# One shared pool of accumulator banks, the two banks of a double declared independent, and a first load in thirds

## The chip, the cores and the metric

The kernel runs on one core of one Trainium2 chip. The metric is device time in microseconds (us) of one execution; a lower time is better. Engines are named as in the profile: PE is the matrix engine (PEld its weight loads), ACT the scalar engine, DVE the vector engine, POOL the general one, SP the one that issues most transfers. Times are medians of several executions; unless said otherwise all were fast. Ratios are the mean time of one kernel's fast runs over the mean of the fast runs of the kernel before in the same rounds, so they are not quite the ratio of the medians quoted.

## The reference

Block-sparse attention (4 batches, 8 heads, 768 tokens, head size 64) feeds a two-layer network with a swish: 512 to 2048 to 512 over 3072 tokens.

```python
scores = (1/sqrt(64)) * q @ k.T                 # per batch and head, 768 x 768
scores = where(mask, scores, -1e9)              # mask: window, first/last, 3 sampled blocks of 32 per row block
attn = softmax(scores);  x = attn @ v           # x: 3072 x 512 after the heads are put side by side
h = x @ w_in                                    # 3072 x 2048
out = (h * sigmoid(beta * h)) @ w_out           # 3072 x 512
```

## The kernel before

All work is cut into nodes. A planner in the kernel (`order_of`) puts them in one order with modelled durations and a weight per kind (`BIAS`); each engine then runs its nodes in that order. So PE's order is fixed when the kernel is built. A "pair" is two heads of one batch; pairs 0 to 3 are batch 0, pair 4 is the first of batch 1. A "score group" is a run of score steps with nothing else between them in PE's order. A "change of form" is a switch of PE between 128-row and 64-row matmuls; each score group costs two, one on entry and one on the way back.

```python
SLOTS = {..., "et": 15, "xst": 7, ..., "sc": 2, "mm": 4}   # 2 doubles + 4 single banks = all 8 banks
"sc": many(psum, "sc", [P, 2, 512], FP32),      # a score step: both heads, one bank each
"mm": many(psum, "mm", [P, 512], FP32),         # all other matmul results
...
def mm(sc=sc, kc0=kc0):                         # a score step: 64-row matmuls, 1024 columns in all
    for i in range(kn):
        for hh in range(2):
            nc.tensor.matmul(at(sc)[:, hh, i*n:(i+1)*n], lhsT=kX[hh*D:(hh+1)*D, ...], rhs=qX[hh*D:(hh+1)*D, ...])
def ex(eng, sc=sc, et=et):                      # one exponential over both banks, frees the double
    nc.scalar.activation(out=at(et)..., in_=at(sc)..., func=AF.Exp, scale=SCALE)
def mk(eng, ...):                               # DVE: et *= mask
...
def hp(f=f, hb=hb):                             # hidden layer: 4 matmuls of 512 columns into one bank
def th(...): tanh on ACT;  def gm(...): (tanh + 1) * h on DVE, frees the bank
def op(...):                                    # out projection: 16 matmuls into one bank, in fours
```

Attention (24 matmuls of 65 columns per bank) is normalized by DVE into `xst`, transposed, and copied to `xT_sb`, from which hidden layers read. A hidden group covers 256 or 512 tokens: 16 nodes of four matmuls. The first full one (512 tokens) needs the attention of all four pairs of batch 0.

The softmax here doesn't subtract the row's maximum and nothing guards it: scores larger than these inputs give would overflow.

## Time and profile before

The median was 280.78 us (280.04 to 281.09, 3 runs).

| | before |
|---|---|
| PE, ACT, DVE busy, share of span | 95%, 76%, 75% |
| PE waits from 63 us to its last matmul | 0.07 us of 213.5 |
| score groups in PE's order (built order) | 78: 14 of one step, 62 of two, 2 of three |
| first exponential | 8.76 us |

From the page of the kernel before: busy time, and two rows of the span in 40 slices (in tenths; PEclk is the clock granted to PE).

```profile
PE 265.3 (95%) x2455; PEld 139.5 (50%) x2455; DVE 209.5 (75%) x424; ACT 212.9 (76%) x281; POOL 28.0 (10%) x45
...
PE   4597899999999999999999999999999999999994
...
PEclk9997799999999999999999999999999999999999
```

The table of windows of the kernel before: for each stretch its length, then busy us of each engine, the clock, the transfer share and rate.

```profile
core 0: us, PE busy (x) PEld busy (x) DVE busy (x) ACT busy (x) POOL busy (x), PEclk, DMA share, GB/s
0.00:63.00 63.00, 51.88 (x573) 31.62 (x573) 52.58 (x128) 49.10 (x67) 13.94 (x29) 0.95 0.97 207
63.00:276.50 213.50, 213.43 (x1884) 107.90 (x1882) 156.91 (x297) 163.22 (x214) 14.02 (x16) 1.00 0.45 109
276.50:280.10 3.60, 0.00 (x0) 0.00 (x0) 0.00 (x0) 0.60 (x1) 0.00 (x0) 1.00 0.20 75
25.00:31.80 6.80, 6.33 (x66) 3.71 (x64) 4.73 (x11) 5.71 (x7) 0.00 (x0) 0.50 1.17 208
```

From 63 us on PE never stops; before that it does, and for 6.8 us it ran at half clock. "Busy" is not "useful", though. PE's timeline in the full stretch (start, length, what, count) shows it:

```profile
84.12 1.89 PE L591 MATMUL mm<-w_out_sb,g 128*128 128x512 f16 x8
85.94 0.60 PE L462 MATMUL sc<-qX,kX 64*128 64x512 f16 x4
86.48 1.90 PE L591 MATMUL mm<-w_out_sb,g 128*128 128x512 f16 x8
88.31 0.60 PE L462 MATMUL sc<-qX,kX 64*128 64x512 f16 x4
88.85 1.90 PE L591 MATMUL mm<-w_out_sb,g 128*128 128x512 f16 x8
```

Eight out-projection matmuls and two score steps repeat every 2.37 us. The eight take 1.727 us (8 x 0.2159, from 48 in a row), the two score steps 0.427 us (the prediction's estimate). The 0.2 us left is put down to the entry into the 64-row form and the way back.

The list of waits (who waited for whom: us in total, times, longest):

```profile
ACT et L470 <- PE sc L462: 22.0, 39, 1.3
...
PE sc L462 <- ACT et L470: 3.0, 7, 0.9
```

The start, from the timeline of all engines. POOL casts k, DVE builds the mask from the sampled indices (`sb_f`), the mask matmul stands first in PE's order, and only then the transposes of k run:

```profile
4.23 0.82 POOL L395 CAST s_k<-st_k 128x768 f16<-128x768 f32 x1 [0.84 <-DMA st_k<-in_k_dram]
4.41 0.66 DVE L287 CAST sb_f<-sb_i 24x3 f32<-24x3 int32 x1 [0.72 <-DMA sb_i<-in_sampled_blocks_dram]
6.01 0.19 PE L294 MATMUL mm<-identity,mask 24*24 24x24 f16 x1 [2.86 <-DVE mask L289]
6.99 0.80 ACT L425 COPY kX<-mm 128x768 f16<-128x768 f16 x1 [3.05 <-PE mm L420]
```

### The profile page before, as it was taken

How to read it: one execution, taken by the hardware profiler on the slowest of the kernel's cores; microseconds unless marked ns; L12 is line 12 of the kernel's file. 1: busy time of each engine (PE TensorE's matmuls, PEld its weight loads, DVE VectorE, ACT ScalarE, POOL GpSimd, SP SyncE). 2: the span in 40 equal slices, each digit the busy share in tenths (PEclk: the TensorE clock that was granted, in tenths of full speed). 3: DMA queues.
4: the chain of work that ended last, by engine and by line, in shares of the span. 5: the costliest groups of instructions: out<-in, count | busy, mean ns of one | idle time of the engine just before them, and what ended most of it. 6: DMA issues, size and time to landing. Idle time of an engine off the chain costs nothing.

```text
span 280.1 us, 6128 instructions
## 1 busy us (share of the span) xinstructions
PE 265.3 (95%) x2455; PEld 139.5 (50%) x2455; DVE 209.5 (75%) x424; ACT 212.9 (76%) x281; POOL 28.0 (10%) x45
## 2 busy tenths in 40 slices
PE   4597899999999999999999999999999999999994
PEld 1364576654363664454563354643355554556741
DVE  5697999999995788887789998877876787733500
ACT  1689898879987898997879988879966877704611
POOL 5560010010200010231001310010000000000000
PEclk9997799999999999999999999999999999999999
DMA  7999994899602194996227986860102010011112
GB/s 204 292 251 213 202 176 115 109 305 233 163 4 37 48 247 115 303 252 150 68 70 204 266 207 86 248 104 35 39 2 77 37 49 37 0 22 75 40 55 96
DMA packets 72849, 36.65 MB, mean 131 GB/s; under 512 B 29796, under 2 KB 68724, under 8 KB 72820
## 3 DMA queue, kind: packets, MB, share of 16 engines
q1 hardware_dynamic: 69568, 32.06, 47.0%
q0 software_dynamic: 3136, 4.19, 8.6%
q8 instruction: 19, 0.31, 0.5%
q14 instruction: 10, 0.08, 0.1%
q10 hardware_dynamic: 116, 0.01, 0.0%
HBM read 27.27 MB, written 6.29 MB: 120 GB/s over the span
## 4 chain that ended last, share of the span: by engine, by line
PE 83%; ACT 7%; DVE 4%; DMA 3%; issue 2%; SPq 0%; ACTq 0%; DVEq 0%
PE mm L591 29%; PE mm L567 28%; PE mm L517 12%; PE sc L462 12%; ACT et L470 5%; DMA st_k<-in_k_dram 2%; PE mm L420 1%; DMA sb_i<-in_sampled_blocks_dram 1%; DVE g L576 1%; DVE et L479 1%; ACT t_sb L572 1%; DVE s_k L395 1%; ACT qX L425 0%; DVE s_q L395 0%; ACT kX L425 0%
## 5 line engine op out<-in xcount | busy, mean ns | idle before, releaser
L470 ACT ACTIVATE et<-sc 128x1024 f16<-128x1024 f32 x144 | 142.2, 1031 | 24.7 <-PE sc L462 22.0
L479 DVE TENSOR_TENSOR et<-et,mask 128x1024 f16<-128x1024 f16 x144 | 98.6, 695 | 20.0 <-ACT et L470 19.7
L591 PE MATMUL mm<-w_out_sb,g 128*128 128x512 f16 x384 | 93.3, 380 | 0.0
L567 PE MATMUL mm<-xT_sb,w_in_sb 128*128 128x512 f16 (+1 forms) x448 | 89.9, 349 | 0.4
L576 DVE SCALAR_TENSOR_TENSOR g<-t_sb,mm 128x512 f16<-128x512 f16 (+1 forms) x112 | 66.0, 608 | 23.3 <-ACT t_sb L572 22.2
L572 ACT ACTIVATE t_sb<-mm,beta_h_sb 128x512 f16<-128x512 f32 (+1 forms) x112 | 67.8, 649 | 12.9 <-PE mm L567 12.1
L567 PEld LDWEIGHTS <-w_in_sb 128*128 128x128 f16 x448 | 42.4, 98 | 44.5 <-issue 6.8
L591 PEld LDWEIGHTS <-g 128*128 128x128 f16 x384 | 33.7, 98 | 43.6 <-issue 11.5
L462 PE MATMUL sc<-qX,kX 64*128 64x256 f16 (+1 forms) x384 | 48.4, 342 | 4.3 <-ACT et L470 3.0
L517 PEld LDWEIGHTS <-et 128*128 128x128 f16 x1152 | 42.3, 100 | 9.2 <-issue 3.1
L517 PE MATMUL mm<-va,et 128*128 128x65 f16 x1152 | 44.5, 196 | 0.0
L462 PEld LDWEIGHTS <-kX 64*128 64x128 f16 x384 | 15.5, 96 | 26.9 <-issue 21.8
L601 ACT ACTIVATE osb<-mm 128x512 f32<-128x512 f32 x16 | 9.6, 599 | 18.9 <-PE mm L591 18.7
L527 DVE TENSOR_TENSOR xst<-mm,recip 128x256 f16<-128x256 f32 x48 | 20.1, 419 | 0.4
L395 POOL CAST s_q<-st_q 128x768 f16<-128x768 f32 (+1 forms) x10 | 8.5, 847 | 92.8 <-DMA st_q<-in_q_dram 89.5
L524 DVE RECIPROCAL recip<-mm 128x4 f32<-128x4 f32 x48 | 8.5, 178 | 5.5 <-PE mm L517 4.9
L395 POOL CAST va<-st_v 128x768 f16<-128x768 f32 x7 | 6.9, 983 | 15.4 <-DMA st_v<-in_v_dram 15.4
L395 DVE CAST s_k<-st_k 128x768 f16<-128x768 f32 x12 | 7.9, 656 | 0.7 <-DMA st_k<-in_k_dram 0.7
L395 DVE CAST va<-st_v 128x768 f16<-128x768 f32 x9 | 4.9, 546 | 1.5 <-DMA st_v<-in_v_dram 1.5
L395 POOL CAST s_k<-st_k 128x768 f16<-128x768 f32 x4 | 3.5, 875 | 20.8 <-DMA st_k<-in_k_dram 20.8
L603 DVE TENSOR_SCALAR osb<-mm 128x512 f32<-128x512 f32 x8 | 5.5, 684 | 0.0
L395 DVE CAST s_q<-st_q 128x512 f16<-128x512 f32 (+2 forms) x10 | 4.5, 454 | 0.0
(53 smaller groups left out, 44.3 us busy)
## 6 DMA issues: line engine op xcount, KB each, us to landing
st_k<-in_k_dram SPq DMA_DIRECT2D x16, 384.0 KB, 4.8
st_v<-in_v_dram SPq DMA_DIRECT2D x16, 384.0 KB, 5.3
out_dram<-osb SPq DMA_DIRECT2D x24, 256.0 KB, 2.0
st_q<-in_q_dram SPq DMA_DIRECT2D x12, 384.0 KB, 4.6
w_in_sb<-in_moe_w_in_dram POOLq DMA_DIRECT2D x2, 1024.0 KB, 12.0
w_out_sb<-in_moe_w_out_dram POOLq DMA_DIRECT2D x2, 1024.0 KB, 21.2
st_q<-in_q_dram SPq DMA_DIRECT2D x12, 128.0 KB, 4.6
xT_sb<-xst SPq DMA_TRANSPOSE x22, 2.4
```

The costliest lines, as they stand in the source:

```text
L395: e(out=at(dst)[:, :, :, 0:D] if nm == "v" else by_chunk(dst, lo, hi), in_=src)
L462: nc.tensor.matmul(at(sc)[:, hh, i * n:(i + 1) * n], lhsT=kX[hh * D:(hh + 1) * D, (kc0 + i) * P:(kc0 + i + 1) * P], rhs=qX[hh * D:(hh + 1) ...
L470: nc.scalar.activation(out=at(et).rearrange("p h q -> p (h q)"), in_=at(sc).rearrange("p h q -> p (h q)"), func=AF.Exp, bias=0.0, scale=SCALE)
L479: nc.vector.tensor_tensor(out=e, in0=e, in1=m, op=ALU.mult)
L517: nc.tensor.matmul(a[:, i, hh, :], lhsT=at(ets[kc // kn])[:, hh, at0:at0 + P], rhs=at(va)[:, hh, kc, 0:D + 1], start=(kc == 0), stop=(kc = ...
L524: nc.vector.reciprocal(out=at(rb), in_=av_ap()[:, :, :, D:D + 1])
L527: nc.vector.tensor_tensor(out=at(xs)[:, half * 2:half * 2 + 2], in0=av_ap()[:, :, :, 0:D], in1=at(rb).to_broadcast([P, 2, 2, D]), op=ALU.mult)
L567: nc.tensor.matmul(at(hb)[:, 0:n], lhsT=w_in_sb[:, c, f * P:(f + 1) * P], rhs=xT_sb[:, c, t0:t0 + n], start=(c == 0), stop=(c == NPAIR - 1))
L572: nc.scalar.activation(out=at(tb)[:, 0:n], in_=at(hb)[:, 0:n], func=AF.Tanh, bias=0.0, scale=beta_h_sb[:, f:f + 1])
L576: nc.vector.scalar_tensor_tensor(out=at(gb)[:, f, 0:n], in0=at(tb)[:, 0:n], scalar=1.0, in1=at(hb)[:, 0:n], op0=ALU.add, op1=ALU.mult)
L591: nc.tensor.matmul(at(ob), lhsT=at(gb)[:, f, ts * P:(ts + 1) * P], rhs=w_out_sb[:, f, :], start=(f == 0), stop=(f == N_FFC - 1))
L601: nc.scalar.activation(out=at(sb), in_=at(ob), func=AF.Copy, bias=0.0, scale=0.5)
```

## The change

Its intent: let score steps use any free double, up to three at once, so that they come in larger groups; let other results use any single bank; and start on the first third of k. The planner gets a pool of eight banks, chooses a bank for each node, and caps what a kind may hold. The buffers' dependency tracking works on the whole double, so every pair of accesses to different banks of a double, on different engines, is declared independent. All weights and several buffer counts were tuned again. The diff, cut to its core:

```diff
-BIAS = {"av": 39, ..., "gm": -151, "hp": 34, ...}
+BIAS = {"av": -69, ..., "gm": -727, "hp": -468, ..., "two sc": -72, ...}
+IN_PARTS = (0,)
+BANKS = ("sc", "mm")
+MOST = {"av": 8, "hp": 6, "sc": 3}
...
+    bank, held = [0.0] * (2 * slots["sc"]), {}      # in order_of: when each bank is free
...
+                b.slot, b.kind = bank_for(bank, b.pool, start), n.kind
...
+class Banks:
+    def access(self, insts, eng, banks, fresh, node=None):
+        for insts2, eng2, gen, node2, own2 in self.seen[d]:
+            if node and node2 and (node2 in before or own & own2):
+                continue
+            if eng2 != eng and not set(gen) & set(banks):
+                for a in insts:
+                    for b in insts2:
+                        self.tc.declare_no_dep(a, b, reason="the other bank of the double")
...
-    SLOTS = {"st_k": 3, "st_q": 6, "st_v": 4, ..., "va": 5, "et": 15, "xst": 7, "recip": 6, "t_sb": 5, ..., "osb": 2, "sc": 2, "mm": 4}
+    SLOTS = {"st_k": 2, "st_q": 5, "st_v": 5, ..., "va": 4, "et": 13, "xst": 5, "recip": 7, "t_sb": 6, ..., "osb": 3, "sc": 4}
...
     def at(buf):
+        if buf.pool == "mm":
+            return T["sc"][buf.slot // 2][:, buf.slot % 2]
...
+        if x in IN_PARTS:                               # first pair: k0, q, k1, k2
+            work = Buf("st_k"), Buf("s16_k")
+            for g in range(NG):
+                parts.append(add_half(x, "k", kq, g * CG, g * CG + CG, ...))
```

Most instructions after it carry one line (L208), that of the helper that records them, so they are told apart by their tiles; every accumulator is now called `sc`.

More of the change, by code (lines that the diff above doesn't have):

```diff
@@ L38, in __init__ @@
         self.start = self.done = self.on = None
-BIAS = {"av": 39, "beta": 625, "cast": 183, "dma": -860, "ex": 395, "gm": -151, "hp": 34,
-        "load": 1245, "lone sc": 160, "mask": -541, "mk": 266, "next sc": -48, "norm": 134,
-        "op": 45, "op on": 85, "osb": 304, "sc": -79, "spread": 28, "th": 302, "turn": -1220,
-        "turn cp": 47, "weights": 444, "x cp": 29, "x turn": -13}
+BIAS = {"av": -69, "beta": -455, "cast": 94, "dma": -1239, "ex": 257, "gm": -727, "hp": -468,
+        "load": 1496, "lone sc": 331, "mask": -1415, "mk": 241, "next sc": 94, "norm": -152,
+        "op": -13, "op on": -70, "osb": 284, "sc": -204, "spread": -316, "th": 422,
+        "turn": -3422, "turn cp": -88, "two sc": -72, "weights": 774, "x cp": -31,
+        "x turn": -102}
 W_GATE = (3, "k")
@@ L54, with banks_of, whole, soonest @@
 SHARED = 42.0
+BANKS = ("sc", "mm")
+MOST = {"av": 8, "hp": 6, "sc": 3}
+def banks_of(b):
+    return (2 * b.slot, 2 * b.slot + 1) if b.pool == "sc" else (b.slot,)
+def whole(bank, d, t):
+    return all(x is not None and x <= t for x in bank[2 * d:2 * d + 2])
+def soonest(bank, pool):
+    if pool == "mm":
+        return min((t for t in bank if t is not None), default=None)
+    pairs = [bank[i:i + 2] for i in range(0, len(bank), 2)]
+    return min((max(p) for p in pairs if None not in p), default=None)
+def bank_for(bank, pool, t):
+    if pool == "sc":
+        ok = [d for d in range(len(bank) // 2) if whole(bank, d, t)]
+        return min(ok, key=lambda d: max(bank[2 * d:2 * d + 2]))
+    ok = [i for i in range(len(bank)) if bank[i] is not None and bank[i] <= t]
+    def other(i):
+        return float("inf") if bank[i ^ 1] is None else bank[i ^ 1]
+    return max(ok, key=lambda i: (other(i), -i))
 def order_of(nodes, free, slots):
     free = dict(free)
-    give = {p: [(0.0, s) for s in range(n)] for p, n in slots.items()}
+    give = {p: [(0.0, s) for s in range(n)] for p, n in slots.items() if p not in BANKS}
+    bank, held = [0.0] * (2 * slots["sc"]), {}
     rows = 128
@@ L81, in order_of @@
             ok = True
+            if held.get(n.kind, 0) >= MOST.get(n.kind, 99):
+                continue
             for p, c in want.items():
+                if p in BANKS:
+                    t = soonest(bank, p)
+                    if t is None:
+                        ok = False
+                        break
+                    ready = max(ready, t)
+                    continue
                 if len(give[p]) < c:
@@ L96, in order_of @@
                         bias += BIAS["next sc"]
-                    elif sum(t <= n_start for t, _ in give["sc"]) < 2:
-                        bias += BIAS["lone sc"]
+                    else:
+                        room = sum(whole(bank, d, n_start) for d in range(len(bank) // 2))
+                        bias += BIAS["lone sc"] if room < 2 else BIAS["two sc"] if room < 3 else 0
                 key = (n_start + n.dur[e] - min(n.dur.values()) + bias, n.place)
@@ L122, in order_of @@
         for b in n.take:
+            if b.pool in BANKS:
+                b.slot, b.kind = bank_for(bank, b.pool, start), n.kind
+                held[n.kind] = held.get(n.kind, 0) + 1
+                for i in banks_of(b):
+                    bank[i] = None
+                continue
             t, b.slot = min(give[b.pool])
@@ L127, in order_of @@
             b.end = max(b.end, n.done)
-            if b.users == 0:
+            if b.users == 0 and b.pool in BANKS:
+                held[b.kind] -= 1
+                for i in banks_of(b):
+                    bank[i] = b.end + HOP
+            elif b.users == 0:
                 give[b.pool].append((b.end + HOP, b.slot))
@@ L139, in order_of, with __init__, __getattr__, call @@
     return out
+class Tap:
+    def __init__(self, eng, log):
+        self.eng, self.log = eng, log
+    def __getattr__(self, name):
+        f = getattr(self.eng, name)
+        def call(*a, **kw):
+            r = f(*a, **kw)
+            self.log.append(r.ins)
+            return r
+        return call
+class Banks:
+    def __init__(self, tc, n):
+        self.tc, self.seen = tc, [[] for _ in range(n)]
+        self.age = [0] * (2 * n)
+    def access(self, insts, eng, banks, fresh, node=None):
+        d = banks[0] // 2
+        if fresh:
+            for i in banks:
+                self.age[i] += 1
+            self.seen[d] = [x for x in self.seen[d]
+                            if any(self.age[i] - g <= 2 for i, g in x[2].items())]
+        own = node and {(b.pool, b.slot) for b in node.use if b.pool not in BANKS}
+        before = node and {m for m, _ in node.deps}
+        for insts2, eng2, gen, node2, own2 in self.seen[d]:
+            if node and node2 and (node2 in before or own & own2):
+                continue
+            if eng2 != eng and not set(gen) & set(banks):
+                for a in insts:
+                    for b in insts2:
+                        self.tc.declare_no_dep(a, b, reason="the other bank of the double")
+        self.seen[d].append((insts, eng, {i: self.age[i] for i in banks}, node, own))
 @with_exitstack
@@ L171 @@
     Q1 = 256
-    SLOTS = {"st_k": 3, "st_q": 6, "st_v": 4, "s16_k": 4, "s16_q": 2, "set": 4, "va": 5,
-             "et": 15, "xst": 7, "recip": 6, "t_sb": 5, "g": 2, "osb": 2, "sc": 2, "mm": 4}
+    SLOTS = {"st_k": 2, "st_q": 5, "st_v": 5, "s16_k": 4, "s16_q": 2, "set": 4, "va": 4,
+             "et": 13, "xst": 5, "recip": 7, "t_sb": 6, "g": 2, "osb": 3, "sc": 4}
     persist = ctx.enter_context(tc.tile_pool(name="persist", bufs=1))
@@ L183 @@
         "sc": many(psum, "sc", [P, 2, 512], FP32),
-        "mm": many(psum, "mm", [P, 512], FP32),
         "et": many(persist, "et", [P, 2, 512], FP16),
@@ L223, in emit_warm @@
                              start=True, stop=True)
+    log = []
+    pe, act, dve = Tap(nc.tensor, log), Tap(nc.scalar, log), Tap(nc.vector, log)
     def copy_on(eng):
-        return nc.scalar.copy if eng == "ACT" else nc.vector.tensor_copy
+        return act.copy if eng == "ACT" else dve.tensor_copy
     sb_i32 = persist.tile([NB, 3], mybir.dt.int32, name="sb_i32")
@@ L286, in mb @@
         def mb(eng):
-            nc.vector.tensor_copy(out=sb_f32, in_=sb_i32)
+            dve.tensor_copy(out=sb_f32, in_=sb_i32)
             for r in range(3):
-                nc.vector.scalar_tensor_tensor(out=mask_blk if r < 2 else mask16, in0=iota_j,
+                dve.scalar_tensor_tensor(out=mask_blk if r < 2 else mask16, in0=iota_j,
                                                scalar=sb_f32[:, r:r + 1], in1=mask_blk,
@@ L293, in mt @@
         def mt():
-            nc.tensor.matmul(at(tb)[0:NB, 0:NB], lhsT=mask16, rhs=identity[0:NB, 0:NB],
+            pe.matmul(at(tb)[0:NB, 0:NB], lhsT=mask16, rhs=identity[0:NB, 0:NB],
                              start=True, stop=True)
@@ L301, in km @@
             for g in range(NG):
-                nc.tensor.matmul(at(kb)[:, g * NB:(g + 1) * NB], lhsT=onehot[:, g], rhs=mask_t,
+                pe.matmul(at(kb)[:, g * NB:(g + 1) * NB], lhsT=onehot[:, g], rhs=mask_t,
                                  start=True, stop=True)
@@ L308, in bt @@
         def bt():
-            nc.tensor.transpose(out=at(bb)[:, 0:N_FFC], in_=beta_sb, identity=ident32)
+            pe.transpose(out=at(bb)[:, 0:N_FFC], in_=beta_sb, identity=ident32)
         def bh(eng):
-            nc.vector.tensor_scalar(out=beta_h_sb, in0=at(bb)[:, 0:N_FFC], scalar1=0.5,
+            dve.tensor_scalar(out=beta_h_sb, in0=at(bb)[:, 0:N_FFC], scalar1=0.5,
                                     scalar2=None, op0=ALU.mult)
         def spread(eng, g):
-            e = nc.vector if eng == "DVE" else nc.gpsimd
+            e = dve if eng == "DVE" else nc.gpsimd
             w = CG * BLK // (CG * CG)
@@ L362, in by_chunk, with add_load @@
         return at(s16)[:, lo * P:hi * P].rearrange("p (c h d) -> p h c d", h=2, d=D)
-    def add_load(nm, x, st, lo, hi, gate):
+    def add_load(nm, x, st, lo, hi, gate, more=False):
         b, j = pairs[x]
@@ L376, in add_load @@
         deps = [(d, -1e9) for d in last_load + begin]
-        kw = {"take": [st]}
+        kw = {"use" if more else "take": [st]}
         if gate is not None:
@@ L384, in add_load, with add_cast @@
         last_load[:] = [add("load", "SP", 500 if hi - lo in (NC, CG) else 1000, 0, load, deps=deps,
-                             moved=68000 * (hi - lo) + (500000 if x == 0 and nm == "v" else 0),
+                             moved=68000 * (hi - lo) + (170000 if x == 0 and nm == "v" else 0),
                              **kw)]
         return last_load[0]
-    def add_cast(x, nm, st, dst, lo, hi, load):
+    def add_cast(x, nm, st, dst, lo, hi, load, more=False):
         w = (hi - lo) * P
         def cast(eng):
-            e = nc.vector.tensor_copy if eng == "DVE" else nc.gpsimd.tensor_copy
+            e = dve.tensor_copy if eng == "DVE" else nc.gpsimd.tensor_copy
             src = at(st)[:, :, lo * D:hi * D].rearrange("p h (c d) -> p h c d", d=D)
@@ L398, in add_cast, with add_half @@
                    deps=[(load, SLACK if x >= NPAIR else 4000 if lo and x == 3 else 0)],
-                   take=[dst], use=[st], port=True)
-    def add_half(x, nm, kq, lo, hi, first, gate):
+                   take=[] if more else [dst], use=[st] + ([dst] if more else []), port=True)
+    def add_half(x, nm, kq, lo, hi, first, gate, at_work=None):
         i = "kq".index(nm)
         w = (hi - lo) * P
-        st, s16 = Buf(f"st_{nm}"), Buf(f"s16_{nm}")
-        load = add_load(nm, x, st, lo, hi, gate)
+        st, s16 = at_work or (Buf(f"st_{nm}"), Buf(f"s16_{nm}"))
+        load = add_load(nm, x, st, lo, hi, gate, at_work and lo > 0)
         if x < NPAIR and lo == 0:
             loads[x, nm] = st, load
-        c = add_cast(x, nm, st, s16, lo, hi, load)
+        c = add_cast(x, nm, st, s16, lo, hi, load, at_work and lo > 0)
         if x >= N_PE_TURN:
@@ L419, in turn @@
             for cc in range(lo, hi):
-                nc.tensor.transpose(out=at(tb).bitcast(FP16)[:, (cc - lo) * P:(cc - lo + 1) * P],
+                pe.transpose(out=at(tb).bitcast(FP16)[:, (cc - lo) * P:(cc - lo + 1) * P],
                                     in_=at(s16)[:, cc * P:(cc + 1) * P],
@@ L433, in add_prep @@
         hi = Q1 // P if x < NPAIR else NC
-        tk = add_half(x, "k", kq, 0, NC, None, gates[0])
-        tq = add_half(x, "q", kq, 0, hi, tk, gates[1])
+        parts = []
+        if x in IN_PARTS:
+            work = Buf("st_k"), Buf("s16_k")
+            for g in range(NG):
+                parts.append(add_half(x, "k", kq, g * CG, g * CG + CG,
+                                      parts[0] if parts else None, None, work))
+                if g == 0:
+                    tq = add_half(x, "q", kq, 0, hi, parts[0], None)
+            tk = parts[0]
+        else:
+            tk = add_half(x, "k", kq, 0, NC, None, gates[0])
+            tq = add_half(x, "q", kq, 0, hi, tk, gates[1])
         lv = add_load("v", x, st, 0, NC, gates[2])
         cv = add_cast(x, "v", st, va, 0, NC, lv)
-        prep[x] = {"kq": kq, "va": va, "k": tk, "q": tq, "q on": tq, "v": cv}
+        prep[x] = {"kq": kq, "va": va, "k": tk, "q": tq, "q on": tq, "v": cv,
+                   "k of": parts or [tk] * NG}
         if x < NPAIR:
@@ L461, in mm @@
                     for hh in range(2):
-                        nc.tensor.matmul(
+                        pe.matmul(
                             at(sc)[:, hh, i * n:(i + 1) * n],
@@ L469, in ex @@
             def ex(eng, sc=sc, et=et):
-                nc.scalar.activation(out=at(et).rearrange("p h q -> p (h q)"),
+                act.activation(out=at(et).rearrange("p h q -> p (h q)"),
                                      in_=at(sc).rearrange("p h q -> p (h q)"),
@@ L478, in mk @@
                     [P, 2 * CG * kn, w])
-                nc.vector.tensor_tensor(out=e, in0=e, in1=m, op=ALU.mult)
-            steps.append((x, q0, sc, et, mm, ex, mk,
+                dve.tensor_tensor(out=e, in0=e, in1=m, op=ALU.mult)
+            k_of = prep[x]["k of"][kc0 // CG:(kc0 + kn - 1) // CG + 1]
+            steps.append((x, q0, k_of, sc, et, mm, ex, mk,
                           [mask_of[g] for g in range(q0 // (CG * P), (q0 + n) // (CG * P))]))
@@ L487, in add_step @@
     def add_step(step, unit):
-        x, q0, sc, et, mm, ex, mk, masks = step
+        x, q0, k_of, sc, et, mm, ex, mk, masks = step
         r = prep[x]
-        g = add("sc", "PE", 218, 180, mm, deps=[(r["k"], SLACK if x >= N_PE_TURN else 0),
+        g = add("sc", "PE", 218, 180, mm, deps=[(t, SLACK if x >= N_PE_TURN else 0)
+                                           for t in dict.fromkeys(k_of)] + [
                       (r["q"] if q0 == 0 else r["q on"], SLACK if x >= N_PE_TURN else 0)],
@@ L516, in av @@
                             at0 = (kc % kn) * n + (qc % CG) * (n // CG) + qc // CG * P
-                            nc.tensor.matmul(
+                            pe.matmul(
                                 a[:, i, hh, :],
@@ L523, in rc @@
             def rc(eng, rb=rb, av_ap=av_ap):
-                nc.vector.reciprocal(out=at(rb), in_=av_ap()[:, :, :, D:D + 1])
+                dve.reciprocal(out=at(rb), in_=av_ap()[:, :, :, D:D + 1])
             def nm(eng, half=half, rb=rb, av_ap=av_ap):
-                nc.vector.tensor_tensor(
+                dve.tensor_tensor(
                     out=at(xs)[:, half * 2:half * 2 + 2], in0=av_ap()[:, :, :, 0:D],
@@ L539, in turn @@
                 for qc in range(nq):
-                    nc.tensor.transpose(out=at(tb).bitcast(FP16)[:, qc * P:(qc + 1) * P],
+                    pe.transpose(out=at(tb).bitcast(FP16)[:, qc * P:(qc + 1) * P],
                                         in_=at(xs)[:, qc].rearrange("p h d -> p (h d)"),
@@ L566, in hp @@
                 for c in range(NPAIR):
-                    nc.tensor.matmul(at(hb)[:, 0:n], lhsT=w_in_sb[:, c, f * P:(f + 1) * P],
+                    pe.matmul(at(hb)[:, 0:n], lhsT=w_in_sb[:, c, f * P:(f + 1) * P],
                                      rhs=xT_sb[:, c, t0:t0 + n],
@@ L571, in th @@
             def th(eng, f=f, hb=hb, tb=tb):
-                nc.scalar.activation(out=at(tb)[:, 0:n], in_=at(hb)[:, 0:n], func=AF.Tanh,
+                act.activation(out=at(tb)[:, 0:n], in_=at(hb)[:, 0:n], func=AF.Tanh,
                                      bias=0.0, scale=beta_h_sb[:, f:f + 1])
             def gm(eng, f=f, hb=hb, tb=tb):
-                nc.vector.scalar_tensor_tensor(out=at(gb)[:, f, 0:n], in0=at(tb)[:, 0:n],
+                dve.scalar_tensor_tensor(out=at(gb)[:, f, 0:n], in0=at(tb)[:, 0:n],
                                                scalar=1.0, in1=at(hb)[:, 0:n],
@@ L590, in op @@
                     for f in range(qq * 4, qq * 4 + 4):
-                        nc.tensor.matmul(at(ob), lhsT=at(gb)[:, f, ts * P:(ts + 1) * P],
+                        pe.matmul(at(ob), lhsT=at(gb)[:, f, ts * P:(ts + 1) * P],
                                          rhs=w_out_sb[:, f, :],
@@ L600, in cp @@
                 if eng == "ACT":
-                    nc.scalar.activation(out=at(sb), in_=at(ob), func=AF.Copy, bias=0.0, scale=0.5)
+                    act.activation(out=at(sb), in_=at(ob), func=AF.Copy, bias=0.0, scale=0.5)
                 else:
-                    nc.vector.tensor_scalar(out=at(sb), in0=at(ob), scalar1=0.5, scalar2=None,
+                    dve.tensor_scalar(out=at(sb), in0=at(ob), scalar1=0.5, scalar2=None,
                                             op0=ALU.mult)
@@ L648 @@
                            "SP": 800.0}, SLOTS)
+    banks = Banks(tc, SLOTS["sc"])
     with tc.manual_schedule():
@@ L652 @@
         for n in seq:
+            log.clear()
             if n.on in ("ACT", "DVE", "POOL") and n.emit.__code__.co_argcount > n_default(n.emit):
@@ L656 @@
                 n.emit()
+            for b in n.use:
+                if b.pool in BANKS:
+                    banks.access(list(log), n.on, banks_of(b), b in n.take, n)
 def n_default(f):
```

## The prediction

> What bounds it now. The page gives PE 95% of the 280.1 us span, ACT 76%, DVE 75%. The table of windows splits it: from 63.0 to 276.5 us PE is busy 213.43 of 213.50 us at full clock, so this stretch is PE's order and nothing else; from 0 to 63 us PE is busy 51.9, partly at half clock (granted clock 0.75 and 0.91 between 20 and 40 us). The tail after PE is 3.6 us. The list of waits charges ACT 22.0 us for score matmuls (39 times) and PE 3.0 us for exponentials.
>
> Inside the full PE stretch not all is matmul. In the timeline from 84 to 92 us, eight out-projection matmuls plus one group of two score steps repeat every 2.37 us. Eight such matmuls take 1.727 us (48 in a row take 10.37), two score steps of 1024 columns 0.427 us (estimate: two row halves at once at that rate), so entering and leaving the 64-row form costs about 0.2 us per group. The Trainium skill, "TensorEngine Tiling (Array Packing)", Key Properties, says that changing the tiling mode drains TensorE; this trace agrees, at about 0.1 us per change.
>
> What the change does. Built order: 2455 matmuls in both, same shapes, so the pure work (about 241 us at these durations) stays. Score steps stand in 78 groups before (14 of one, 62 of two, 2 of three) and 55 after (21 of two, 34 of three): with four doubles three scores can be in flight. Hidden layers, formerly cut in pieces of 4 to 20, become solid runs of 64. 23 fewer groups x 0.2 us = 4.6 us, nearly all on the chain. Eight short POOL/ACT pieces are added by the split of the first k.
>
> Start: the first exponential begins at 8.76 us, after a 0.80 us copy of all of k and a 0.38 us copy of q. In thirds these overlap: about 0.7 us earlier. The mask matmul at 6.0 us still stands in front, which caps this. Until about 35 us ACT paces, with gaps of 0.7 to 1.7 us where only two score buffers exist; a third should recover 1 to 3 us, unless DMA (a 5.65 us load for batch 1 is on the chain at 50 us) takes it back.
>
> Costs: between the solid hidden runs ACT must do more. A repeating 5-score pattern is 5.0 us on PE (16 matmuls, 5 steps, 2 groups) against 5 x 0.95 us of exponentials plus one latency, 95 to 100%; in a hidden run, 16 activations of 0.64 us leave 3.6 of 13.8 us, which three waiting scores fill. New PE waits on exponentials are likely, 1 to 3 us in all. Fewer st_k, xst and et buffers may cost a little.
>
> Sum: 280.8 - 4.6 - 0.7 - 2 + 1 = about 274.5 us; range 269.5 to 279.5. Faster by over 2%: 0.57; within 2%: 0.39; slower: 0.04.
>
> What would show it: score groups each costing 0.2 us as before, with PE fully busy from about 60 us to near the end; first exponential at about 8.0 us; ACT's waits on scores well under 22 us; half of the gain already won at the end of the first batch. Wrong if: PE's waits on exponentials exceed 4 us in the list of waits; waits on t_sb or g inside hidden runs; the second half of w_in, now issued later from POOL, stalling the first hidden run near 30 us; a longer half-clock interval because PE is sparser early; or waits left between the two banks of a double, seen as PE waiting for work on the other bank.

## The result, and the profile after

276.81 us median (276.63 to 278.25, 4 runs) against 280.67 us (4 runs): ratio 0.9876, 95% interval 0.9837 to 0.9914. It is faster, by 1.2%, so within 2%; 274.5 us had been forecast.

The page after:

```profile
PE 259.7 (94%) x2455; PEld 139.7 (51%) x2455; DVE 209.2 (76%) x416; ACT 217.1 (79%) x284; POOL 32.5 (12%) x53
...
PE   6677899969999999999999999999999999999993
...
PEclk9999999999999999999999999999999999999999
```

The windows after, with the same columns, cut where the first full hidden run starts and where the last matmul ends:

```profile
0.00:61.10 61.10, 50.06 (x585) 31.69 (x586) 52.09 (x126) 52.81 (x73) 16.05 (x34) 1.00 0.94 213
61.10:270.70 209.60, 209.58 (x1870) 108.03 (x1869) 157.10 (x291) 163.67 (x212) 16.43 (x19) 1.00 0.47 112
270.70:275.00 4.30, 0.03 (x1) 0.00 (x0) 0.00 (x0) 0.60 (x1) 0.00 (x0) 1.00 0.17 63
```

PE is again full from about 61 us on. The span is 5.1 us shorter than in the first profile of the kernel before, more than the 3.9 us between the timed medians; the half-clock interval of that profile is the reason to be careful here (experiment c1_before). PE's timeline, at the same kind of place:

```profile
83.08 1.89 PE L208 MATMUL sc<-w_out_sb,g 128*128 128x512 f16 x8
84.90 0.82 PE L208 MATMUL sc<-qX,kX 64*128 64x512 f16 x6
85.65 1.90 PE L208 MATMUL sc<-w_out_sb,g 128*128 128x512 f16 x8
87.48 0.61 PE L208 MATMUL sc<-qX,kX 64*128 64x512 f16 x4
88.02 1.70 PE L208 MATMUL sc<-va,et 128*128 128x65 f16 x48
...
61.12 13.97 PE L208 MATMUL sc<-xT_sb,w_in_sb 128*128 128x512 f16 x64 [0.58 <-DVE xT_sb L208]
```

Groups of three (six matmuls) and two alternate. The hidden run is one piece: 64 matmuls in 13.97 us, 0.218 us each, with no gap. The waits after:

```profile
ACT et L208 <- PE sc L208: 13.4, 19, 1.4
...
PE sc L208 <- ACT et L208: 2.4, 6, 0.5
```

The start after: everything is earlier, also the sampled indices, which the change doesn't touch.

```profile
3.26 0.17 DVE L208 CAST sb_f<-sb_i 24x3 f32<-24x3 int32 x1 [0.34 <-DMA sb_i<-in_sampled_blocks_dram]
3.43 0.39 POOL L497 CAST s_k<-st_k 128x256 f16<-128x256 f32 x1
4.44 0.19 PE L208 MATMUL sc<-identity,mask 24*24 24x24 f16 x1 [0.17 <-DVE mask L208]
5.84 0.65 ACT L208 COPY kX<-sc 128x256 f16<-128x256 f16 x2
6.86 2.85 ACT L208 ACTIVATE et<-sc 128x1024 f16<-128x1024 f32 x3 [0.38 <-PE sc L208]
```

To see where time went I kept a ledger for each trace. Every matmul is given the time that it takes in a full row at full clock (0.2159 us for 512 columns, 256 in proportion; 0.762 us for 24 attention matmuls; 0.2135 us for a score step, an estimate; transposes 0.07; the five tiny matmuls of the start 1.3 us together). The sum is 240.9 us in every kernel here. A matmul's start minus the work ordered before it is the time PE has lost by then: waits, half clock and changes of form together. The ledger compares kernels at equal work, whatever their order. For two profiles without the half-clock interval (c1_before is the kernel before profiled again, c0_after the changed kernel again; spans 278.4 and 274.4 us; their granted clock reads 1.00 until PE's last matmul, but see the last point of this document on the first 16 to 18 us):

| PE work done, us | lost before, us (changes of form) | lost after | difference |
|---|---|---|---|
| 0 to 10 | 15.50 (15) | 12.51 (11) | -2.99 |
| 10 to 20 | 3.83 (15) | 3.93 (7) | +0.10 |
| 20 to 30 | 1.38 (12) | 0.59 (6) | -0.79 |
| 30 to 40 | 1.50 (10) | 3.68 (10) | +2.18 |
| 40 to the last matmul | 11.41 (104) | 8.38 (76) | -3.03 |
| last matmul's start to end of span | 4.08 | 4.68 | +0.60 |

The gain sits in two places: at the very start, and in the full stretch. In the rest of batch 0 (work 10 to 40), where 14 changes of form fell away, PE lost 1.5 us more. Two limits of the ledger: with the five tiny matmuls charged by their columns, the first row's difference is 2.3 us and not 3.0 (summed up to 20 us of work it is 2.9 to 3.3 either way, and up to 40 us it stays 1.5); and the first profile of the changed kernel had lost 21.31 us at 40 us of work where c0_after had lost 20.71, so two profiles of one kernel differ by 0.6 us in batch 0.

### The profile page after: what moved, and what is told of

Its sections match the earlier page's. It is cut to its first block, busy times and chain, and to the rows that moved or that the text cites. A ratio compares the mean times of both kernels' runs of the same rounds, so it can differ in the third digit from the quotient of the medians.

```text
span 275.0 us, 6172 instructions
## 1 busy us (share of the span) xinstructions
PE 259.7 (94%) x2455; PEld 139.7 (51%) x2455; DVE 209.2 (76%) x416; ACT 217.1 (79%) x284; POOL 32.5 (12%) x53
## 4 chain that ended last, share of the span: by engine, by line
PE 88%; DVE 5%; ACT 2%; DMA 2%; SPq 1%; issue 1%; ACTq 0%; DVEq 0%
PE sc L208 88%; DVE et L208 2%; ACT et L208 2%; DMA st_k<-in_k_dram 2%; DVE xst L208 1%; SPq L477 1%; DVE recip L208 0%; DVE kX L208 0%; DVE s_k L208 0%; DVE xT_sb L208 0%; ACT qX L208 0%; ACT osb L208 0%; SPq L474 0%; DVE s_q L208 0%; DVE qX L208 0%
## 5 line engine op out<-in xcount | busy, mean ns | idle before, releaser
L208 ACT ACTIVATE et<-sc 128x1024 f16<-128x1024 f32 x144 | 136.4, 1045 | 13.9 <-PE sc L208 13.4
L208 DVE TENSOR_TENSOR et<-et,mask 128x1024 f16<-128x1024 f16 x144 | 94.8, 693 | 8.1 <-ACT et L208 8.0
L208 PE MATMUL sc<-w_out_sb,g 128*128 128x512 f16 x384 | 90.0, 379 | 0.0
L208 PE MATMUL sc<-xT_sb,w_in_sb 128*128 128x512 f16 (+1 forms) x448 | 84.3, 349 | 1.1 <-DVE xT_sb L208 1.0
L208 ACT ACTIVATE t_sb<-sc,beta_h_sb 128x512 f16<-128x512 f32 (+1 forms) x112 | 68.2, 649 | 17.1 <-PE sc L208 17.1
L208 DVE SCALAR_TENSOR_TENSOR g<-t_sb,sc 128x512 f16<-128x512 f16 (+1 forms) x112 | 67.6, 611 | 16.0 <-ACT t_sb L208 15.6
L208 PEld LDWEIGHTS <-w_in_sb 128*128 128x128 f16 x448 | 43.8, 98 | 40.7 <-issue 1.5
L208 PEld LDWEIGHTS <-g 128*128 128x128 f16 x384 | 34.6, 98 | 43.2 <-issue 7.5
L208 PE MATMUL sc<-qX,kX 64*128 64x256 f16 (+1 forms) x384 | 44.0, 339 | 4.7 <-ACT qX L208 1.9
L208 PEld LDWEIGHTS <-et 128*128 128x128 f16 x1152 | 39.7, 98 | 9.7 <-issue 6.6
L208 PE MATMUL sc<-va,et 128*128 128x65 f16 x1152 | 42.4, 194 | 1.1 <-ACT et L208 1.0
L208 PEld LDWEIGHTS <-kX 64*128 64x128 f16 x384 | 16.4, 98 | 26.5 <-issue 19.2
L208 ACT ACTIVATE osb<-sc 128x512 f32<-128x512 f32 x18 | 11.0, 608 | 17.9 <-PE sc L208 17.9
L208 DVE TENSOR_TENSOR xst<-sc,recip 128x256 f16<-128x256 f32 x48 | 20.3, 424 | 1.8 <-DVE recip L208 0.2
L497 POOL CAST s_k<-st_k 128x768 f16<-128x768 f32 (+1 forms) x11 | 8.2, 753 | 76.7 <-DMA st_k<-in_k_dram 76.6
L208 DVE RECIPROCAL recip<-sc 128x4 f32<-128x4 f32 x48 | 8.7, 180 | 10.4 <-PE sc L208 8.7
L497 POOL CAST s_q<-st_q 128x768 f16<-128x768 f32 (+2 forms) x11 | 9.0, 821 | 33.4 <-DMA st_q<-in_q_dram 33.0
L208 DVE CAST va<-st_v 128x768 f16<-128x768 f32 x9 | 5.0, 558 | 0.9 <-DMA st_v<-in_v_dram 0.9
L208 PE MATMUL sc<-identity,s_k 128*128 128x128 f16 x24 | 3.5, 305 | 2.0 <-DVE s_k L208 1.2
L208 DVE CAST s_k<-st_k 128x768 f16<-128x768 f32 x7 | 3.9, 554 | 1.4 <-issue 0.7
L208 DVE COPY xT_sb<-sc 128x256 f16<-128x256 f16 (+1 forms) x9 | 3.1, 346 | 1.8 <-PE sc L208 1.8
```

Source lines behind the costliest of these rows:

```text
L208: r = f(*a, **kw)
L497: e(out=at(dst)[:, :, :, 0:D] if nm == "v" else by_chunk(dst, lo, hi), in_=src)
```

## The experiments

Theory: in the full stretch each change of form costs PE 0.11 us, and 28 fewer are the gain there; in batch 0 PE isn't the limit, so fewer changes and a third score buffer could gain nothing, and only the earlier start counts. Rivals: the gain is only the start; or only the new order; or fewer waits, not fewer changes. All experiments edit the changed kernel unless said otherwise.

### c0_after and c1_before: both kernels again

> Control: the changed kernel again, on the chip that runs the experiments beside it. Both theories expect the ratio on record, 0.988 (0.984 to 0.991), about 277 us. Beside it I read the granted clock of the runs of the kernel before: if the runs of the kernel before show 1.00 and still 280.5 us, the half-clock interval in its profile is not what the gain in the profile pair (5.1 us against 3.5 to 3.9 us timed) owed its surplus to.

> Control: the kernel before again, with a profile of its own, to see whether its half-clock interval (25 to 32 us in the first profile, granted clock 0.988) is there in every execution. In the seven runs beside the first experiments it was there in part: clocks 0.988 to 1.000 with spans 280.3 to 278.3 us. Expected: ratio 1.00, clocks again spread over 0.988 to 1.000, and in the profile PE slower between 20 and 40 us only where the clock says so.

c0_after: 277.06 us, ratio 0.9864 (0.9825 to 0.9904). c1_before: 280.3 us, ratio 0.9981 (0.9944 to 1.0018). In the seven runs of the kernel before beside c0_after the mean granted clock went from 0.988 (spans 280.1 and 280.3 us) to 1.000 (278.3 us); the control's four runs had 0.997 to 1.000. So the half-clock interval comes and goes, is worth up to 2 us, and fell mostly on the kernel before. Two profiles free of it differ by 3.9 us, but c0_after's was the fastest of its four runs. Over all rounds, the runs with a mean clock of 0.997 or more average 280.3 us before (16 runs) and 276.9 us after (7 runs), so without the interval the gain is about 3.5 us.

### e1_nodecl: without the declarations

```diff
-                        self.tc.declare_no_dep(a, b, reason="the other bank of the double")
+                        pass
```

> The changed kernel with the same order on every engine (the listing is identical), only the declarations left out, so that two banks of a double count as one buffer. Theory A: the pool is worth something only because of the declarations; inside the solid hidden runs a matmul into one bank must now wait for the activation and the multiply of the bank beside it, so the hidden runs open up by several tenths of a us per pair of tiles: 56 pairs x 0.3 to 1 us, 295 to 330 us, with long waits of PE on DVE and ACT. Rival B: the order is what counts and the waits are short enough to hide: under 280 us.

337.41 us, ratio 1.2012, with the identical order on every engine. From its list of waits:

```profile
PE sc L208 <- DVE g L208: 23.4, 40, 1.7
PE sc L208 <- DVE xst L208: 9.0, 13, 1.8
```

Theory A holds, and the cost was above even its range: 60 us. A part of it is clock and not waiting: the four runs had mean clocks of 0.975 to 0.990. Two banks in one buffer are one bank unless the program says otherwise. That they may be used at once agrees with the Trainium skill, "PSUM — Partial Sum Buffer", section "PSUM bank collisions raise a hardware error", which says that engines on different banks run clean: the results of c0_after were correct.

### e2_wholek and e9_loads_in_parts: the first k whole again

Same order; the part nodes emit nothing and the third emits the whole. e9 gives the load back its thirds and leaves cast, transposes and copy whole.

```diff
         def cast(eng):
+            if x in IN_PARTS and nm == "k":
+                if hi_ < NC: return
+                lo, hi = 0, NC            # the same in turn and cp; in e2 also in load, with the first part
```

> The changed kernel with the same order except that the first k is loaded, cast, transposed and copied in one piece at the place of its third part (mask matmul first, then q, then k). Theory A (the time won at the start survives to the end in part): first exponential later by about 1.5 us, at 8.0 to 8.8 us, and the total 0.5 to 1.5 us longer than the control. Rival B: ACT's saturated stretch at 51 to 61 us swallows it: first exponential as late, total within 0.4 us of the control. Rival C: the whole gain of the change is in the start: total 3 us or more longer.

> The whole-k experiment with the first k's load alone in thirds again (cast, transposes and copy still in one piece): separates the size of the load from the pipelining on the engines. In the three profiles with a whole first load the cast of the sampled block indices began at 4.40 to 4.42 us, in the four with thirds at 3.26 to 3.55, and the mask matmul at 6.0 to 6.2 against 4.4 to 5.3 us. Theory A (the large load in front delays the small index load, and with it the mask that stands first in PE's order): indices cast by 3.6 us, mask matmul by 5.1 us, first exponential at 7.8 to 8.4 us in place of 9.16. Rival B (index load lands late for another reason): cast at 4.4 us, first exponential at 8.9 us or later.

e2: 277.66 us, ratio 0.9890 (0.9857 to 0.9923); e9 (another chip): 278.2 us, 0.9910 (0.9870 to 0.9951). The start of e2, then of e9:

```profile
4.42 0.16 DVE L208 CAST sb_f<-sb_i 24x3 f32<-24x3 int32 x1 [1.49 <-DMA sb_i<-in_sampled_blocks_dram]
6.17 0.19 PE L208 MATMUL sc<-identity,mask 24*24 24x24 f16 x1 [3.02 <-DVE mask L208]
9.16 1.02 ACT L208 ACTIVATE et<-sc 128x1024 f16<-128x1024 f32 x1 [0.71 <-PE sc L208]
```

```profile
3.42 0.16 DVE L208 CAST sb_f<-sb_i 24x3 f32<-24x3 int32 x1 [0.49 <-DMA sb_i<-in_sampled_blocks_dram]
4.43 0.19 PE L208 MATMUL sc<-identity,mask 24*24 24x24 f16 x1 [1.27 <-DVE mask L208]
8.54 1.94 ACT L208 ACTIVATE et<-sc 128x1024 f16<-128x1024 f32 x2 [0.71 <-PE sc L208]
```

The first load's size alone brings the index load in 1.0 us sooner and the mask matmul 1.7 us sooner: theory A of e9. The first exponential moves less than it said, 0.62 us, because the whole k's copy (0.80 us) now gates it; the thirds on the engines bring the other 1.5 us (7.02 in c0_after). The Trainium skill, "DMA: Bandwidth & Descriptors", section "Issuing engines are not separate DMA queues", says that transfers of several issuing engines run on the same 16 DMA engines and interleave; that agrees with a small load held up by a large one issued at the same time. e2 starts 2.14 us later than c0_after and is 1.96 us behind at 40 us of work and at the last matmul (lost 22.67 against 20.71, 31.05 against 29.09). Against that profile the shift passes through unchanged; against the first profile of the changed kernel, which starts 2.30 us before e2, 1.36 us is left at both places. In times it is smaller: 0.6 us in the medians, as the control's four spans scatter from 274.4 to 276.0 us, and the two intervals overlap; e9's lead over e2 was gone at 40 us of work (22.61). So rival C falls, and rival B (batch 0 swallows the shift) is not excluded. I put the thirds at 0.6 to 2 us and leave it there.

### e3_split: the same work with 99 score groups

Where nothing it needs stands between, the matmul node after a group of scores is put ahead of the group's last step.

```diff
+    seq = split_scores(seq)     # ... sc sc sc op ...  becomes  ... sc sc op sc ...
     banks = Banks(tc, SLOTS["sc"])
```

> The changed kernel where one out-projection, attention or hidden node that follows a group of scores is put ahead of the group's last step, wherever nothing it needs stands between: 99 score groups in place of 55, otherwise the same work, buffers and order. Theory A (each group costs two changes of form, 0.1 us each, on PE's full stretch): 0.2 us x 44 = 8.8 us at most, 6 to 9 us longer than the control, about 284 us, PE still fully busy after 62 us. Rival B (groups don't matter, the gain comes from fewer waits): within 1.5 us of the control.

286.95 us, ratio 1.0220 (1.0183 to 1.0257); 9.9 us over the control, a little above theory A's range. The ledger from 40 us of work to the last matmul:

| kernel | changes of form | lost, us | us per change |
|---|---|---|---|
| c0_after | 76 | 8.38 | 0.110 |
| c1_before | 104 | 11.41 | 0.110 |
| e3_split | 152 | 17.06 | 0.112 |

Three orders, one price. It can also be read directly: in the full stretch of c0_after a score matmul starts 0.312 us after a 512-column matmul, where two of the latter start 0.216 us apart, so the entry alone costs 0.096 us (medians). The ledger's 0.110 is a little high because score steps inside a group start 0.22 us apart and not the 0.2135 charged. PE was full there in e3 too, but for 0.48 us of 218; without these, its 76 changes more than the control's cost 0.108 us each:

```profile
63.60:281.60 218.00, 217.52 (x1870) 106.37 (x1868) 158.60 (x291) 165.89 (x212) 17.80 (x19) 1.00 0.43 105
```

Before 40 us of work e3 lost 2.84 us more than the control for 12 more changes. That part says nothing on the price: this profile had a half-clock interval there (granted clock 0.70 from 25 to 30 us, 0.95 over the first 63.6 us, 1.00 in the control), worth up to 3.2 us (estimate: 0.05 x 63.6), and it includes waits.

### e4_oldpool_newbias and e5_newpool_oldbias: half of the change each

e4 is the kernel before with the new `BIAS`; e5 the changed kernel with the old one ("two sc" set to 0).

> The kernel before with only the order's weights exchanged for those of the changed kernel (old pool of two doubles and four single banks, old buffers, first k whole). Built order: 64 score groups in place of 78. Theory A (fewer groups are worth 0.2 us each only if the exponentials keep up; two doubles can't feed groups of three to six without waits): slower than the kernel before, by 2 to 25 us, with PE waiting for exponentials more than 10 us. Rival B (the gain is the retuned order, not the pool): faster than the kernel before by 1 to 3 us.

> The changed kernel with the order's weights of the kernel before (new pool, declarations and buffers kept, first k in thirds). Built order: 74 score groups, many of one. Theory A (the pool alone is worth nothing without an order that uses it): no faster than the kernel before, 279 to 292 us. Rival B (the pool frees PE by itself): faster than the kernel before, near 277 us.

e4: 302.61 us, ratio 1.0784; e5: 293.32 us, ratio 1.0436, 1.3 us above its range. Theory A holds in both: the order alone, or the pool alone, is much slower than either full kernel. In e4 two doubles can't feed the groups asked for:

```profile
PE sc L463 <- ACT et L471: 15.3, 32, 0.9
```

That doesn't apportion the gain, since weights are fitted to a pool; it shows that neither half can be kept alone with these weights. The other buffer counts that changed (`et`, `xst` and so on) went with the pool and were not tested on their own.

### e6_lessdve, e7_lessact, e8_both: what held the first full hidden run

PE's timeline after, before that run:

```profile
54.15 0.38 PE L208 MATMUL sc<-identity,xst 128*128 128x128 f16 x4
54.85 0.63 PE L208 MATMUL sc<-qX,kX 64*128 64x512 f16 x4 [0.32 <-ACT et L208]
55.76 0.39 PE L208 MATMUL sc<-qX,kX 64*128 64x512 f16 x2 [0.29 <-ACT et L208]
56.68 1.68 PE L208 MATMUL sc<-va,et 128*128 128x65 f16 x48 [0.52 <-ACT et L208]
58.30 0.61 PE L208 MATMUL sc<-qX,kX 64*128 64x256 f16 x8
59.82 0.40 PE L208 MATMUL sc<-qX,kX 64*128 64x256 f16 x4 [0.91 <-DVE xst L208]
```

These scores belong to batch 1 and stand ahead of, or between, what the hidden run waits for. e6 leaves out 12 mask multiplies of pairs 2 and 3; e7 takes 12 exponentials there over one head; e8 is e6 plus half exponentials for pair 4. All three give wrong results.

```diff
             def mk(eng, et=et, kc0=kc0):
+                if x in (2, 3) and q0 == Q1: return                      # e6, e8
...
             def ex(eng, sc=sc, et=et):
+                if x in (2, 3) and q0 == Q1:                             # e7;  in e8: if x == 4
+                    act.activation(out=at(et)[:, 0, :], in_=at(sc)[:, 0, :], ...); return
```

> The changed kernel, same order, with the 12 mask multiplies of pairs 2 and 3 in the second part of batch 0 left out (wrong result on purpose): 12 x 0.62 = 7.4 us less work for DVE just before the first full hidden run, which started at 60.6 to 61.1 us. Theory A (in batch 0 DVE paces, 94% busy from 20 to 60 us, so fewer changes of form and a third score buffer could not help there): the first full hidden run starts 2 to 4 us earlier and the total falls by as much, 273 to 275 us. Rival B (ACT paces, 95% busy): within 0.7 us of the control's 277. Rival C (PE's waits for shared banks pace): within 0.7 us too.

> The changed kernel, same order, with the 12 exponentials of the same steps done over one head in place of two (wrong result on purpose): about 12 x 0.43 = 5 us less for ACT, DVE's work unchanged. Theory A (DVE paces that stretch): the first full hidden run starts less than 1 us earlier, total within 1 us of the control's 277. Rival B (ACT paces): 2 to 4 us earlier, and the total with it.

> Neither less DVE work nor less ACT work alone moved the start of the first full hidden run (60.7, 61.3 us beside 60.6 to 61.1). The traces show why it could: in PE's order six scores of pair 4 stand ahead of the attention of pair 3, PE waits for their doubles at the pace of one exponential each, and the attention's bank lies in a double that still holds one of them (0.52 us wait); at the same time DVE's multiplies of pair 3 end only just before. So two limits end within 0.5 us of each other. This kernel relieves both, in the same order: the mask multiplies of the experiment before are left out, and the exponentials of pair 4 are done over one head (wrong result on purpose). Theory A (both limits together): the first full hidden run starts 1.3 to 2.5 us earlier than with less DVE work alone, at 58.2 to 59.4 us, and the total is shorter than 276.5 us by about as much. Rival B (something else, such as loads or the transposes of pair 4, paces): no earlier than 60.3 us, total within 0.5 us.

e6: 276.49 us (0.9853); e7: 276.89 us (0.9868); e8: 275.69 us (0.9818). My theory that DVE paces fell, and so did ACT at that place: with 7.4 us less on DVE, or about 5 us less on ACT, the hidden run began at 60.70 and 61.26 us, beside 60.52 (control) and 61.12 us in the two profiles of the unedited kernel. In e6 and then e8 the attention of pair 3 and the hidden run:

```profile
56.97 1.68 PE L208 MATMUL sc<-va,et 128*128 128x65 f16 x48 [0.52 <-ACT et L208]
60.70 1.67 PE L208 MATMUL sc<-xT_sb,w_in_sb 128*128 128x512 f16 x7 [0.58 <-DVE xT_sb L208]
```

```profile
56.18 1.70 PE L208 MATMUL sc<-va,et 128*128 128x65 f16 x48
59.92 3.40 PE L208 MATMUL sc<-xT_sb,w_in_sb 128*128 128x512 f16 x15 [0.58 <-DVE xT_sb L208]
```

In e6 the attention still waits 0.52 us for an exponential, though it needs none of pair 4's: its bank lies in a double that a score of batch 1 held (the built order puts it into both banks of the double that the third of pair 4's scores had). In e8 that wait is gone and the run starts 0.78 us sooner; between 30 and 40 us of work PE lost 2.52 us, against 3.58 in e6 and 3.68 in the control. That is the direction of theory A of e8 and less than its 1.3 us. So 1.1 us of the loss there came from batch 1's scores, taken in front of batch 0's attention and in its bank (pair 4's exponentials were shortened only together with the multiplies, so this is shown of the two together; it is one profile, and two of the unedited kernel differ by 0.6 us in this stretch; which part is the bank and which the place in the order is not shown). Of the 2.5 us left, ten changes of form are 1.1 us at 0.11; the rest, with short waits for the normalize, transpose and copy in a row, is read and not tested.

### f1_vlate: an attempt to beat both

The second pair's k and q are loaded before the first v, and the weights are searched anew with the kernel's planner (54 score groups, 38 of three).

```diff
+V_LATE = (0,)
-    for x in range(NPAIR): add_prep(x)
+    late = None
+    for x in range(NPAIR):
+        now = add_prep(x)          # for x in V_LATE: k and q now, v returned for later
+        if late: late()
+        late = now
```

> A version meant to beat both: the changed kernel with the second pair's k and q loaded ahead of the first v (the second k's cast waited for its load until 8.3 us while ACT ran out at 9.7), and the order's weights searched anew with the kernel's own planner. Built order: 54 score groups, 38 of three, and only four scores between the last attention of batch 0 and the first full hidden run in place of nine. From the ledger of the traces: 1 to 2 us less lost before the first full hidden run, one group fewer; 275.0 to 276.5 us against 277. If the planner's finer gains are not real on the chip: within 0.5 us of the changed kernel.

276.92 us, ratio 0.9849 (0.9813 to 0.9885): the same as the changed kernel. By the ledger PE had lost 1.38 us more than the control at 10 us of work (13.89 against 12.51), won most of it back by 40 (21.02 against 20.71), and stayed behind. The planner's plan was a gain that the chip didn't show.

## Why the prediction was right or wrong

Direction and range held (276.81 in 269.5 to 279.5); the size did not, and "faster by over 2%", given 0.57, didn't come. Point by point, with the ledger of c1_before and c0_after:

- "entering and leaving the 64-row form costs about 0.2 us per group": right. 0.110 us per change of form in three kernels with 76, 104 and 152 changes.
- "23 fewer groups x 0.2 us = 4.6 us, nearly all on the chain": this step failed in "nearly all". The full stretch has 28 of the 46 fewer changes and shows 3.03 us. The others lie in batch 0, where the profile shows no gain: from 10 to 40 us of work 14 changes fell away and PE lost 1.5 us more.
- "a third [score buffer] should recover 1 to 3 us": failed. ACT's waits on scores fell from 22.0 to 13.4 us as said (20.4 to 13.3 in c1_before and c0_after), but the hidden run that ends batch 0 came no sooner for it; the lead at 10 us of work, 2.99 us, had shrunk to 1.50 at 40 (0.90 with the first profile of the changed kernel). e8 shows where 1.1 us of it went: attention waited behind scores of batch 1, and for a bank in a double that one of them held.
- "about 0.7 us earlier" at the start: too small; the first exponential came 1.9 us earlier. "The mask matmul at 6.0 us still stands in front" was the wrong reading: it moved to 4.4 us, because the index load had been held up by the large first load (e9).
- New waits of 1 to 3 us between the hidden runs: none. PE waited 0.02 us of 209.6, and its six waits on exponentials, 2.4 us, all lie in batch 0 (20.7 to 57 us).
- w_in's second half stalling the first hidden run: no; that run's 64 matmuls took 7.38 us in one piece from 30.18 us. A longer half-clock interval: the opposite; it was rarer after.
- Half of the gain at the end of batch 0: a third (1.5 of 4.5 us at the last matmul).

The sum that was forecast, 4.6 + 0.7 + 2 - 1, measured as 3.0 (full stretch) + 3.0 (start) - 1.5 (rest of batch 0) - 0.6 (tail) = 3.9 us in profiles, 3.5 to 4.1 us in timed runs. The tail's 0.6 us is not explained: it is the last output's transfer, and e2, with the same order there, had the short one (4.0 us). Some of the agreement is luck: the start gave 2.3 us more than forecast, partly by a route that the prediction had ruled out (the mask matmul's), and made up for a part of the 3.5 us that batch 0 missed; without this surplus the sum would be 1.6 us, and the time about 279.1, near the upper end of the range.

## What to carry to other kernels

Price a change in PE's order by the stretch in which PE is full: count the changes of form there, at about 0.1 us each here, and promise nothing for those in stretches that a chain of other engines paces (here 14 fewer showed no gain; no experiment took them out alone). A shared pool frees buffers only where dependencies are tracked per bank, and it lets early work take the bank that urgent work needs next; look for waits of the urgent work on results that it doesn't use. Near the start, ask which small load stands behind a large one.

## What the Trainium skill lacked or had wrong

- "TensorEngine Tiling (Array Packing)", Key Properties, says that a change of tiling mode drains TensorE and gives no price: 0.110 to 0.112 us per change here, between 128-row and 64-row matmuls, over 76 to 152 changes.
- "DMA: Bandwidth & Descriptors" says that the queues interleave on the same engines, packet by packet, and gives no figure for what a large load does to a tiny one issued beside it. Here a 0.3 KB index load landed in time for a cast at 4.32 to 4.42 us beside a 384 KB first load (four profiles), and at 3.26 to 3.64 us beside a 128 KB one (ten profiles).
- "TensorE: Matmul & The Clock Gate", section "Seeing it yourself", warns that clock events in traces can be unreliable. It holds here in one more way: the granted clock reads 1.00 from 10 to 20 us of the first profile before, while 24 attention matmuls at 14.20 us took 1.50 us, as long as in the interval that reads 0.50, and 0.94 us at 19.73 us. The changed kernel has the same (1.53 us at 13.19, 0.93 at 21.04 in its first profile), so both sides of the comparison start slow.
